# A shift for the softmax: from a row of bounds, made by matmuls of their own, to sixteen rows of the scores' contraction

## The chip, the core and the metric

The kernel runs on one core of one Trainium2 chip, with one launch. The metric is the device time of one execution in microseconds (us). The kernel before took 1345.86 us (median of 3 runs, 1345.21 to 1346.31).

## What is computed

One block mixes two branches over the same input x (2048 tokens, 512 channels) by a gate per token:

```python
x = A_x
g = sigmoid((x * gate_w).sum(-1, keepdims=True))
# branch A: attention, H = 32 heads of Dh = 16
q, k, v = split_heads(x @ wqkv)
p = softmax(einsum("bhqd,bhkd->bhqk", q, k) * Dh ** -0.5)
a = (p @ v, heads joined) @ wo
# branch B: an MLP over the token axis
h = layernorm(x)
b = (gelu(h^T @ w1 + b1) @ w2 + b2)^T        # hidden width F = 1792
out = g * a + (1 - g) * b
```

Everything is float32 with a float32 result. The kernel gets that precision from a faster float format by splitting each operand in a high and a low part and adding three products: high by high, high by low, low by high.

## The kernel before

**Stages.** The program runs five stages after each other, each of them a stretch of the profile.

1. *v and the gate* (0 to 65 us). Tiles of x are loaded, transposed on TensorE, split (`turn`) and multiplied with the v columns of `wqkv`. The gate comes from a row sum on VectorE.
2. *Projection* (65 to 153 us). For each of four blocks b of 128 channels (8 heads), `project` makes k and then q, transposed: 128 channels by 512 tokens in one PSUM bank, 12 matmuls each (L72), for n = 0 to 3. So there are 32 units: 16 of k and 16 of q. `parts` splits each unit in `pc` (ScalarE copies the high part, VectorE subtracts for the low part) and stores both planes to DRAM (`kp`, `qp`; `pc` has three buffers). In between, VectorE makes the layer norm of eight tiles of x for branch B (`ln_load`, `ln_scale`, `ln_rows`).
3. *First layer of the MLP* (153 to 314 us): `layer` (L360), with weights split just ahead of their use on ScalarE and GpSimd, and `gelu` on VectorE and ScalarE.
4. *Attention* (319 to 1290 us), with the second MLP layer and the output projection woven in. The order of all engines is written out by hand here. A group is a pair of heads by half of the queries: 32 groups, some 30 us each. A group has 11 phases (`ph`). In one phase TensorE makes six scores (`score`, L706: 128 keys by 512 queries), beside them up to six matmuls of the dense work (`dn`, L744), and then 24 products with v of the phase before (`apply_v`, L673). ScalarE turns two scores at a time into exponentials (L715). VectorE takes finished `dn` banks out (L442, L551), takes the finished sum of a group out (`evacuate`), and divides attention outputs (`divide` in `fetch_o`: it waits for the loads `o_lo` and `o_sum`, L527 and L528). There is a single bank for `dn` and a single one for `av`.
5. *The end* (1290 to 1345 us): the last output rows.

**Scores.** A score contracts the stacked planes of one head in one half of the 128 rows (`HALF` = 64): 16 rows each of high k by high q, high k by low q and low k by high q (`PAIRS`). One row more (`C_ROW`) takes a shift off, so that no exponential overflows without a look at the scores themselves: on the side of k this row holds ones, on the side of q the shift of each query, 49 rows in all.

**The shift.** It is a bound of what a query can reach with any key: minus 1.01 times the sum over the head's 16 channels of |q| times the greatest |k| of the channel. `kmax` (L312) holds the greatest |k| for each channel of a block, `km` (L315) places it in one column per head, `qa` (L322) is |q| in bf16, and `bound` (L294 to L301) multiplies the two on TensorE: 128 rows, 8 heads, 512 queries, one matmul for each q unit (L296). VectorE copies the 8 by 512 result to `cb` (L297) and reduces its least value into `far` (L299); `cb` goes to DRAM as `cd`. Bounds run late: a list `late` keeps them back until three are waiting, and `last_bounds` does the rest after the first block of the MLP's first layer. `far` then gives a flag (L343 to L348) that decides at the very end (L816) whether a slow general softmax has to run instead; it doesn't on these inputs.

**Loads in attention.** `load_q` (at phase 0) and `load_k` (at phase 1) fetch the next group's operands into two buffers each: six DMAs of 128 KB for k (`ks<-kp`, L422), six of 64 KB for q (`qs<-qp`, L422) and two of 4 KB for the shift (`qs<-cd`, L437). All are issued by SyncE (SP) in program order, with every other load and store of the kernel in the same queue: the weights (`w_raw`, L133), outputs of a group (`o`, L647, and `r`, L657), `o_lo` and `o_sum`, and rows of branch B (`row`, L547). The rows of ones in the two k buffers are set once by four memsets on VectorE (L413), just ahead of the first attention loads.

The order in stages 1 to 3 is made by a scheduler from program order and data dependences; an instruction's place on its engine can thus move when others go.

Of the kernel before, what the change touches and what calls it, by code (L numbers as in the profile page):

```python
# [21 lines left out]
P = 128  # L22
# [19 lines left out]
PAIRS = [(0, 0, 0), (DH, 0, 1), (2 * DH + 1, 1, 0)]  # L42
C_ROW = 2 * DH
ROWS = DH * len(PAIRS) + 1
# [13 lines left out]
def gated_mix(ctx: ExitStack, tc: tile.TileContext, a_x, a_wqkv, a_wo, b_w1, b_b1, b_w2, b_b2, gate_w, out):  # L58
# [18 lines left out]
    qp_d = [dram.tile([2, P, S], F32, name=f"qp{b}") for b in range(ND)]  # L77
    kp_d = [dram.tile([2, P, S], F32, name=f"kp{b}") for b in range(ND)]
    c_d = [dram.tile([P // DH, S], F32, name=f"cd{b}") for b in range(ND)]
# [12 lines left out]
    far = const.tile([P // DH, ND * NQ], F32, name="far")  # L92
# [187 lines left out]
    with tc.tile_pool(name="ln0", bufs=3, side="right") as ln:  # L280
# [8 lines left out]
        def parts(ps, dst, n):  # L289
            pc = qk.tile([P, 2, NB], F32R, name="pc", bufs=3)  # L290
            split(pc[:, 0, :], pc[:, 1, :], ps, nc.scalar.copy, nc.vector.tensor_tensor)
            nc.sync.dma_start(dst[:, :, n * NB : (n + 1) * NB].rearrange("c p t -> p c t"), pc.bitcast(F32))

        def bound(b, n, km, qa, cb):  # L294
            pc = bank()[: P // DH]
            nc.tensor.matmul(pc, km, qa, start=True, stop=True)  # L296
            nc.vector.tensor_copy(cb[:, n * NB : (n + 1) * NB], pc)  # L297
# [5 lines left out]
        late = []  # L303
        for b in range(ND):
            wk_b, wq_b = qk_w.pop(0), qk_w.pop(0)
            kmax = bd.tile([P, NQ], F32, name="kmax")
            for n in range(NQ):
# [3 lines left out]
                parts(ps, kp_d[b], n)  # L311
                nc.vector.tensor_reduce(kmax[:, n : n + 1], ps, axis=AX.X, op=ALU.max, apply_absolute_value=True)  # L312
            nc.vector.tensor_reduce(kmax[:, 0:1], kmax, axis=AX.X, op=ALU.max)
            km = bd.tile([P, P // DH], BF16, name="km")
            nc.vector.tensor_scalar(km, head_of, kmax[:, 0:1], BOUND_SLACK, ALU.mult, ALU.mult)  # L315
            cb = bd.tile([P // DH, S], F32R, name="cb", bufs=1)
            for n in range(NQ):
                ps = project(wq_b, n)
                while len(late) > 2:
                    bound(*late.pop(0))  # L320
# [573 lines left out]
```

## Time and profile before

| | us |
|---|---|
| median of 3 runs | 1345.86 |
| the profiled execution | 1346.53 |
| its span, first to last instruction | 1344.7 |
| busy ScalarE (ACT) | 1093.5 |
| busy VectorE (DVE) | 421.2 |
| busy GpSimd (POOL) | 202.2 |
| TensorE weight loads (PEld, beside matmuls) | 773.1 |
| TensorE clock granted, mean | 0.997 of full speed |
| DMA moved | 133.16 MB, 99 GB/s over the span |

All terms of the prediction are taken from the profiled execution, which is 0.67 us above the median of the runs.

How to read the rows: in a view of *groups*, a row is a line of the code, an engine, an operation, its output and inputs by name, shapes and a count, then the busy time in us with the mean of one in ns, then the engine's idle time ahead of it and what ended that. In a *timeline* a row starts with the start and the duration in us; an idle time and its releaser stand in brackets at the end. SPq rows are DMA issues, not transfers. Matmuls overlap: one of 512 columns is shown with 0.39 us, and the next starts 0.23 us after it. A row of *windows* gives for a stretch the busy time of PE, PEld, DVE, ACT and POOL with instruction counts, then the granted clock, the share of the 16 DMA engines that was busy, and GB/s.

### The profile page before, as it was taken

The numbers are of one execution on the slowest core, as the hardware profiler recorded it, in microseconds if no ns is written. First come the engines' busy times: TensorE is split into PE (matmuls) and PEld (weight loads), VectorE is DVE, ScalarE is ACT, GpSimd is POOL, SyncE is SP. The second block draws the span as 40 slices with busy tenths as digits, with TensorE's granted clock in tenths as the row PEclk, the third lists the DMA queues.
The fourth block names the chain that finished last, engine by engine and source line by source line (L and its number), as shares of the span: only waits on it lengthen the run. The fifth ranks groups of instructions, "written<-read, shape, count | busy, mean of one in ns | idle before, by whom it ended". The sixth has DMA issues, their size and how long they took to land.

```text
span 1344.7 us, 32450 instructions
## 1 busy us (share of the span) xinstructions
PE 1321.9 (98%) x13302; PEld 773.1 (57%) x13302; DVE 421.2 (31%) x637; ACT 1093.5 (81%) x1264; POOL 202.2 (15%) x458
## 2 busy tenths in 40 slices
PE   8999999999999999999999999999999999999996
PEld 6877788876555555555555555555555555554543
DVE  3596663444321111112322111232111122333223
ACT  3353244446999999999999999999999999999994
POOL 0210144443110111111100111100111111100001
PEclk9999999999999999999999999999999999999998
DMA  3565443326432333333555332454333333456411
GB/s 117 164 235 207 169 142 94 94 63 150 88 76 53 73 69 60 71 67 64 115 120 125 80 78 46 102 131 116 69 69 62 73 69 64 90 127 177 93 29 66
DMA packets 90776, 133.16 MB, mean 99 GB/s; under 512 B 13381, under 2 KB 52443, under 8 KB 87515
## 3 DMA queue, kind: packets, MB, share of 16 engines
q1 hardware_dynamic: 90186, 130.21, 39.7%
q8 instruction: 107, 1.75, 0.6%
q10 hardware_dynamic: 432, 0.79, 0.2%
q14 instruction: 51, 0.41, 0.1%
HBM read 97.01 MB, written 33.94 MB: 97 GB/s over the span
## 4 chain that ended last, share of the span: by engine, by line
PE 91%; issue 4%; ACT 1%; DVE 1%; DMA 1%; POOL 0%; SPq 0%; POOLq 0%; DVEq 0%; ACTq 0%
PE av L673 33%; PE s L706 26%; PE acc L360 11%; PE acc L72 10%; PE dn L744 10%; ACT pt L715 1%; DMA o_sum<-r 1%; PE acc L184 1%; PE acc L296 0%; DVE ks L413 0%; DMA wv_raw<-in_A_wqkv_dram 0%; POOL base L805 0%; SPq L422 0%; DVE o_sum L531 0%; POOL w_lo L65 0%
## 5 line engine op out<-in xcount | busy, mean ns | idle before, releaser
L715 ACT ACTIVATE pt<-s 128x1024 f32<-128x1024 f32 x1024 | 965.0, 1031 | 38.8 <-PE s L706 33.1
L706 PE MATMUL s<-qs,ks 49*128 49x512 f32 x2048 | 530.9, 421 | 4.0 <-ACT pt L715 4.0
L673 PE MATMUL av<-pt,v 128*17 128x256 f32 x8192 | 510.6, 381 | 0.1
L706 PEld LDWEIGHTS s<-qs,ks 49*128 49x128 f32 x2048 | 303.8, 184 | 208.5 <-ACT pt L715 157.2
L673 PEld LDWEIGHTS av<-pt,v 128*17 128x17 f32 x8192 | 205.2, 97 | 258.5 <-issue 124.4
L744 PE MATMUL dn<-u_hi,w_hi 64*128 64x512 f32 x432 | 186.1, 431 | 0.6 <-POOL token L748 0.6
L65 POOL TENSOR_TENSOR w_lo<-w_raw,w_hi 128x512 fp32r<-128x512 f32 (+1 forms) x128 | 155.1, 1215 | 143.4 <-ACT w_hi L64 113.3
L744 PE MATMUL dn<-u_lo,w_hi 64*128 64x512 f32 x432 | 171.2, 396 | 0.0
L744 PE MATMUL dn<-u_hi,w_lo 64*128 64x512 f32 x432 | 169.7, 393 | 0.0
L748 POOL MEMSET token<- 1x1 f32 x310 | 28.3, 91 | 848.6 <-PE dn L744 584.7
L639 DVE COPY ot<-av 128x512 f32<-128x512 f32 x32 | 22.1, 691 | 354.8 <-PE av L673 354.8
L652 DVE RECIPROCAL rt<-rt 128x512 f32<-128x512 f32 x31 | 103.9, 3353 | 1.1
L64 ACT CAST w_hi<-w_raw 128x512 fp32r<-128x512 f32 (+1 forms) x67 | 37.9, 567 | 69.7 <-PE acc L360 63.7
L360 PE MATMUL acc<-h_hi,w_lo 128*128 128x512 f32 x224 | 88.7, 396 | 0.3 <-POOL w_lo L65 0.3
L360 PE MATMUL acc<-h_hi,w_hi 128*128 128x512 f32 x224 | 88.9, 397 | 0.0
L360 PE MATMUL acc<-h_lo,w_hi 128*128 128x512 f32 x224 | 88.6, 395 | 0.0
L744 PEld LDWEIGHTS dn<-u_hi,w_lo 64*128 64x128 f32 x432 | 79.8, 185 | 5.2
L744 PEld LDWEIGHTS dn<-u_hi,w_hi 64*128 64x128 f32 x432 | 79.5, 184 | 4.8 <-POOL token L748 1.0
L744 PEld LDWEIGHTS dn<-u_lo,w_hi 64*128 64x128 f32 x432 | 80.0, 185 | 2.5
L64 DVE CAST w_hi<-w_raw 128x512 fp32r<-128x512 f32 (+1 forms) x61 | 22.5, 378 | 116.0 <-PE dn L744 79.6
L442 DVE TENSOR_SCALAR row<-dn,b2x,omg 128x512 f32<-128x512 f32 x16 | 12.9, 809 | 126.9 <-PE dn L744 105.9
L72 PE MATMUL acc<-xt_hi,wc_hi 128*128 128x512 f32 x128 | 51.2, 400 | 0.0
(133 smaller groups left out, 1076.7 us busy)
## 6 DMA issues: line engine op xcount, KB each, us to landing
w_raw<-in_B_w_dram SPq DMA_DIRECT2D x96, 256.0 KB
ks<-kp SPq DMA_DIRECT2D x192, 128.0 KB
qs<-qp SPq DMA_DIRECT2D x192, 64.0 KB
x<-in_A_x_dram SPq DMA_DIRECT2D x32, 256.0 KB
kp<-pc SPq DMA_DIRECT2D x16, 512.0 KB
qp<-pc SPq DMA_DIRECT2D x16, 512.0 KB
w_raw<-in_B_w_dram SPq DMA_DIRECT2D x32, 128.0 KB
bp<-row SPq DMA_DIRECT2D x16, 256.0 KB
```

What stands on the lines that cost most here:

```text
L64: copy(hi, src)
L65: sub(lo, src, hi.bitcast(F32), ALU.subtract)
L72: nc.tensor.matmul(ps, a, b, start=start and n == 0, stop=stop and n == last)
L184: nc.tensor.transpose(pt[:, k, :], xs[t][:, k * P : (k + 1) * P], ident)
L360: nc.tensor.matmul(p, a, b, start=first and k == 0, stop=last and k == 2)
L639: nc.vector.tensor_copy(ot, av)
L652: nc.vector.reciprocal(rt, rt)
L673: nc.tensor.matmul(av[32 * j : 32 * j + VC, i * QC : (i + 1) * QC], v[:, c, g % NP * 2 + i, :], pt[:, h * QC : (h + 1) * QC], start=added[ ...
L706: nc.tensor.matmul(s[:, m, :], kt[grp][rows, c * P : (c + 1) * P], qt[grp][rows, qb * NB : (qb + 1) * NB], start=True, stop=True,)
L715: nc.scalar.activation(pt, s, AF.Exp, scale=SCALE)
L744: mm = nc.tensor.matmul(ps, a[half], b[half], start=first and not second, stop=last and bool(second))
L748: fence = nc.gpsimd.memset(token, 0.0)
```

## The change

The row of ones and the row of shifts go. The three pairs of planes take 48 rows, and 16 rows more (`SHIFT`) hold |q| on the side of q and the greatest |k| of the channel, times -1.01, on the side of k, the same value for all keys. So the score's own contraction takes the shift off: 64 rows in place of 49, a full half.

- In the projection, `bound` and its 16 matmuls go, with `qa`, `cb`, `cd` and the list `late`. |q| becomes a third plane of `pc` and `qp`: ScalarE writes it there in the same activation (Abs), after VectorE's low part, and the store of a q unit grows from 512 KB to 768 KB. VectorE reduces the greatest |q| of each channel (`qmax`), 128 by 512 from PSUM, once for each q unit.
- For each block, VectorE scales `kmax` and spreads it to 128 by 512 (`km`), which is stored to DRAM (256 KB).
- The flag is made from `most` (greatest |q| times greatest |k| for each channel and block) by two small matmuls in `least_shifts`, in the place of `last_bounds`: 8 by 4 and 1 by 4. TensorE gets to the first of them 14 matmuls into the MLP's first layer, and to the second 2 full matmuls later.
- In attention, `load_k` issues two DMAs more, 128 KB each, which repeat 2 KB of `km` four times in each of 16 rows; `load_q` fetches the third plane by two DMAs of 64 KB in the place of the two of 4 KB. The k buffers come from the pool like the q buffers; the four memsets go.
- The general softmax reads the same planes as before.

```diff
-PAIRS = [(0, 0, 0), (DH, 0, 1), (2 * DH + 1, 1, 0)]
-C_ROW = 2 * DH
-ROWS = DH * len(PAIRS) + 1
+PAIRS = [(0, 0, 0), (DH, 0, 1), (2 * DH, 1, 0)]
+SHIFT = (3 * DH, 2, 2)
+ROWS = 4 * DH
...
-        def parts(ps, dst, n):
-            pc = qk.tile([P, 2, NB], F32R, name="pc", bufs=3)
+        def parts(ps, dst, n, m):
+            pc = qk.tile([P, 3, NB], F32R, name="pc", bufs=3)[:, :m, :]
             split(pc[:, 0, :], pc[:, 1, :], ps, nc.scalar.copy, nc.vector.tensor_tensor)
+            if m == 3:
+                nc.scalar.activation(pc[:, 2, :], ps, AF.Abs)
             nc.sync.dma_start(dst[:, :, n * NB : (n + 1) * NB].rearrange("c p t -> p c t"), pc.bitcast(F32))
 
-        def bound(b, n, km, qa, cb):
-            pc = bank()[: P // DH]
-            nc.tensor.matmul(pc, km, qa, start=True, stop=True)
-            nc.vector.tensor_copy(cb[:, n * NB : (n + 1) * NB], pc)
-            i = b * NQ + n
-            nc.vector.tensor_reduce(far[:, i : i + 1], pc, axis=AX.X, op=ALU.min)
-            if n == NQ - 1:
-                nc.sync.dma_start(c_d[b], cb.bitcast(F32))
+        def greatest(dst, ps):
+            nc.vector.tensor_reduce(dst, ps, axis=AX.X, op=ALU.max, apply_absolute_value=True)
...
             nc.vector.tensor_reduce(kmax[:, 0:1], kmax, axis=AX.X, op=ALU.max)
-            km = bd.tile([P, P // DH], BF16, name="km")
-            nc.vector.tensor_scalar(km, head_of, kmax[:, 0:1], BOUND_SLACK, ALU.mult, ALU.mult)
-            cb = bd.tile([P // DH, S], F32R, name="cb", bufs=1)
+            nc.vector.tensor_scalar_mul(kmax[:, 0:1], kmax[:, 0:1], BOUND_SLACK)
+            km = bd.tile([P, NB], F32R, name="km")
+            nc.vector.tensor_copy(km, kmax[:, 0:1].broadcast_to([P, NB]))
+            nc.sync.dma_start(km_d[b], km.bitcast(F32))
             for n in range(NQ):
                 ps = project(wq_b, n)
-                while len(late) > 2:
-                    bound(*late.pop(0))
-                qa = bd.tile([P, NB], BF16, name="qa", bufs=4)
-                nc.scalar.activation(qa, ps, AF.Abs)
-                parts(ps, qp_d[b], n)
-                late.append((b, n, km, qa, cb))
+                parts(ps, qp_d[b], n, 3)
+                greatest(qmax[:, n : n + 1], ps)
...
+            nc.vector.tensor_reduce(qmax[:, 0:1], qmax, axis=AX.X, op=ALU.max)
+            nc.vector.tensor_mul(most[:, b : b + 1], qmax[:, 0:1], kmax[:, 0:1])
...
-    def last_bounds():
-        while late:
-            bound(*late.pop(0))
-
-        nc.vector.tensor_scalar(far, far, -BOUND_LIMIT, None, ALU.is_lt)
-        pf = bank()[:1, : ND * NQ]
+    def least_shifts():
+
+        ps = bank()
+        nc.tensor.matmul(ps[: P // DH, :ND], head_of, most, start=True, stop=True)
+        far = bd.tile([P // DH, ND], F32, name="far")
+        nc.vector.tensor_scalar(far, ps[: P // DH, :ND], -BOUND_LIMIT, None, ALU.is_lt)
+        pf = bank()[:1, :ND]
         nc.tensor.matmul(pf, ones[: P // DH, :], far, start=True, stop=True)
...
-    k_bufs = [stk.tile([P, S], F32R, name=f"ks{i}", bufs=1) for i in range(2)]
-    for t in k_bufs:
-        for i in range(2):
-            nc.vector.memset(t[i * HALF + C_ROW : i * HALF + C_ROW + 1].bitcast(F32), 1.0)
-
-    def stack(dst, src, which, pair, cols):
+    def stack(dst, src, which, pair, cols, planes):
         b, r0 = divmod(pair * 2 * DH, P)
         for i in range(2):
-            for row, *part in PAIRS:
+            rows = slice(r0 + i * DH, r0 + (i + 1) * DH)
+            for row, *part in planes:
                 at = slice(i * HALF + row, i * HALF + row + DH)
-                rows = slice(r0 + i * DH, r0 + (i + 1) * DH)
                 nc.sync.dma_start(dst[at].bitcast(F32), src[b][part[which], rows, cols])
+            if which:
+                at = slice(i * HALF + SHIFT[0], i * HALF + SHIFT[0] + DH)
+                shift = km_d[b][rows][:, None, :].broadcast_to([DH, NQ, NB])
+                nc.sync.dma_start(dst[at].bitcast(F32).rearrange("r (n c) -> r n c", c=NB), shift)
 
     def load_k(g):
-        t = k_bufs[g % 2]
-        stack(t, kp_d, 1, g % NP, slice(0, S))
+        t = stk.tile([P, S], F32R, name="ks")
+        stack(t, kp_d, 1, g % NP, slice(0, S), PAIRS)
         return t
 
     def load_q(g):
...
-        stack(t, qp_d, 0, pair, cols)
-        b, h0 = divmod(pair * 2, P // DH)
-        for i in range(2):
-            at = i * HALF + C_ROW
-            nc.sync.dma_start(t[at : at + 1].bitcast(F32), c_d[b][h0 + i : h0 + i + 1, cols])
+        stack(t, qp_d, 0, pair, slice(half * QW, (half + 1) * QW), [*PAIRS, SHIFT])
         return t
```

More of the change, by code (lines that the diff above doesn't have):

```diff
@@ L91, in gated_mix @@
     omg = const.tile([P, NS], F32, name="omg")
-    far = const.tile([P // DH, ND * NQ], F32, name="far")
+    most = const.tile([P, ND], F32, name="most")
     flag = const.tile([1, 1], I32, name="flag")
@@ L394, in gated_mix @@
                 if f0 == 0 and c == 0:
[L395 removed]
+                    least_shifts()
                 if f0 == 0 and c == 1:
@@ L813, in gated_mix @@
     att_ctx.close()
-    far_off = nc.values_load(flag, min_val=0, max_val=(P // DH) * ND * NQ, skip_runtime_bounds_check_because="a count")
+    far_off = nc.values_load(flag, min_val=0, max_val=H, skip_runtime_bounds_check_because="a count")
     with tc.If(far_off != 0):
```

22 lines of the change are left out of this document (9 added, 13 removed).

## The prediction

> **What bounds the kernel now.** I read the page's busy times first, then the chain of work that ended last, then the groups, and last the timeline at the places where the change acts.
>
> ```profile
> span 1344.7 us, 32450 instructions
> PE 1321.9 (98%) x13302; PEld 773.1 (57%) x13302; DVE 421.2 (31%) x637; ACT 1093.5 (81%) x1264; POOL 202.2 (15%) x458
> PE av L673 33%; PE s L706 26%; PE acc L360 11%; PE acc L72 10%; PE dn L744 10%; ACT pt L715 1%; DMA o_sum<-r 1%; PE acc L184 1%; PE acc L296 0%; DVE ks L413 0%; DMA wv_raw<-in_A_wqkv_dram 0%; POOL base L805 0%; SPq L422 0%; DVE o_sum L531 0%; POOL w_lo L65 0%
> ```
>
> TensorE is busy for 98% of the span, and the chain runs nearly always through it. So a matmul that goes is worth its slot, and work on another engine is free unless TensorE comes to wait for it. The chain has small links that the change touches: the bounds (L296), the memsets (L413), and a load (`o_sum`).
>
> **The bounds go.** First what one costs, from the timeline of TensorE in the projection:
>
> ```profile
> 80.83 0.39 PE L72 MATMUL acc<-xt_hi,wc_lo 128*128 128x512 f32 x1
> ...
> 81.15 0.38 PE L296 MATMUL acc<-qa,km 128*8 128x512 bf16 x1
> ...
> 81.46 0.50 PE L72 MATMUL acc<-xt_hi,wc_hi 128*128 128x512 f32 x1
> ...
> 81.80 0.40 PE L72 MATMUL acc<-xt_lo,wc_hi 128*128 128x512 f32 x1
> ...
> 82.03 0.39 PE L72 MATMUL acc<-xt_hi,wc_lo 128*128 128x512 f32 x1
> ```
>
> The undisturbed pitch is 0.23 us (81.80 to 82.03). From 80.83 to 82.03 lie 1.20 us with three full matmuls, 0.69 us, so one bound takes 0.51 us, twice its place, because the matmuls on both sides of it start late as well. Thirteen of the sixteen stand alone like this: 13 x 0.51 = 6.6 us. Three stand together after the first block of the MLP's first layer:
>
> ```profile
> 155.83 0.40 PE L360 MATMUL acc<-h_hi,w_lo 128*128 128x512 f32 x1
> 156.16 0.81 PE L296 MATMUL acc<-qa,km 128*8 128x512 bf16 x3
> 156.90 0.50 PE L360 MATMUL acc<-h_hi,w_hi 128*128 128x512 f32 x1
> 157.24 0.40 PE L360 MATMUL acc<-h_lo,w_hi 128*128 128x512 f32 x1
> ```
>
> From 155.83 to 157.24 lie 1.41 us with two full matmuls, 0.46 us: the three cost 0.95 us. **Term 1: -7.6 us**, on the path, as TensorE has no idle time in this stage (44.00 busy of 44.00 in the row of windows further down).
>
> **VectorE and ScalarE.** These are not on the path here.
>
> ```profile
> L297 DVE CAST cb<-acc 8x512 fp32r<-8x512 f32 x16 | 10.8, 673 | 7.8 <-PE acc L296 6.4 <-DMA cd<-cb 1.4
> ...
> L312 DVE TENSOR_REDUCE kmax<-acc 128x1 f32<-128x512 f32 x16 | 10.8, 677 | 0.0
> ...
> L322 ACT ACTIVATE qa<-acc 128x512 bf16<-128x512 f32 x16 | 9.5, 595 | 15.9 <-PE acc L72 15.9
> ```
>
> `qmax` has the shape of `kmax`, 677 ns x 16, and replaces the copy alone (673 ns x 16); the reduction to `far` goes on top, and four copies to `km` come. ScalarE's Abs stays and only writes another tile. What hides all this are eight PSUM banks ahead of TensorE; without them VectorE's order would cost time. The memsets stand in the chain too:
>
> ```profile
> 310.42 1.76 DVE L413 MEMSET ks<- 1x2048 f32 x1 [0.47 <-issue]
> ...
> 311.48 0.39 PE L360 MATMUL acc<-h_hi,w_lo 128*128 128x512 f32 x1
> ...
> 312.21 1.41 DVE L368 TENSOR_SCALAR gu<-acc,b 128x512 f32<-128x512 f32 x2
> ```
>
> The first `gu` needs the bank that was finished at 311.48 + 0.39 and so could start 0.3 us earlier. I take 0, as the start of attention is set by loads (below), and -0.3 as the bound.
>
> **The flag's matmuls.** One small matmul becomes two.
>
> ```profile
> 162.14 0.39 PE L360 MATMUL acc<-h_lo,w_hi 128*128 128x512 f32 x1
> ...
> 162.59 0.50 PE L360 MATMUL acc<-h_hi,w_lo 128*128 128x512 f32 x1
> 162.93 0.39 PE L360 MATMUL acc<-h_hi,w_hi 128*128 128x512 f32 x1
> ```
>
> The present one costs 0.79 - 0.46 = 0.33 us; one more costs the same. The first now waits for `most`, behind which all of TensorE's queue stands. Its chain from the last projection's end: ScalarE's high part, VectorE's low part, ScalarE's Abs, VectorE's `qmax` and two tiny operations. At 0.60 us an operation for ScalarE (L322) and 0.68 for VectorE (L312) these are 2.6 us; with some 0.3 us for the tiny ones and 0.39 us until the last matmul is through, that is 3.3 us and some handovers; TensorE gets there after 14 matmuls x 0.23 = 3.2 us. I take 0.2 us, with bounds of 0 and 1. The second small matmul has two full matmuls and its neighbour's delay to cover one tiny VectorE operation: nothing. **Term 2: +0.5 us.**
>
> **The scores.** A score gets 64 rows in place of 49.
>
> ```profile
> L706 PE MATMUL s<-qs,ks 49*128 49x512 f32 x2048 | 530.9, 421 | 4.0 <-ACT pt L715 4.0
> L706 PEld LDWEIGHTS s<-qs,ks 49*128 49x128 f32 x2048 | 303.8, 184 | 208.5 <-ACT pt L715 157.2
> ...
> L744 PEld LDWEIGHTS dn<-u_hi,w_lo 64*128 64x128 f32 x432 | 79.8, 185 | 5.2
> ```
>
> The dense work beside the scores has 64 rows already: its weights load in 185 ns against 184, and on the timeline the two kinds of matmul start together, 0.23 us apart. So nothing, from 0 to 1 ns x 2048 = 2 us if the load were exposed, which it isn't.
>
> **The loads.** Here the change pays. Each group loads 2 x 131 kB more for k and 2 x 62 kB more for q, 12 MB over the 32 groups. Most of it is far from any wait, since operands are asked for a whole group, some 30 us, ahead. The places that matter are those where TensorE stands behind a transfer that now queues behind the new ones.
>
> ```profile
> 65.00:109.00 44.00, 44.00 (x188) 33.84 (x187) 40.38 (x117) 20.91 (x44) 5.92 (x4) 1.00 0.71 247
> ...
> 308.00:318.00 10.00, 8.80 (x39) 6.89 (x38) 9.14 (x11) 4.51 (x8) 5.55 (x5) 1.00 0.87 171
> 668.00:685.00 17.00, 16.91 (x206) 8.66 (x208) 4.38 (x4) 16.81 (x19) 1.82 (x7) 1.00 0.78 154
> ```
>
> From 668 to 685 the engines moved 154 GB/s at a share of 0.78: 197 GB/s at full share. The two new k loads, 262 kB, then take 1.3 us of a queue that is full. That is my price per place, between 0 (other transfers leave room) and 2.2 us (0.9 us of SP's time for two issues, as six take 2.73 us below, comes on top).
>
> First place, the second fetch of attention outputs:
>
> ```profile
> 669.52 2.73 SPq L422 DMA_DIRECT2D ks<-kp  x6
> ...
> 684.37 1.22 DVE L531 TENSOR_TENSOR o_sum<-o_lo,o_sum 128x1024 f32<-128x1024 f32 x1 [12.59 <-DMA o_sum<-r]
> ...
> 688.46 0.47 PE L744 MATMUL dn<-wo_hi,o_hi 64*128 64x512 f32 x1 [0.58 <-DVE row L442]
> ```
>
> VectorE waits 12.59 us for `o_sum`, issued right behind the k loads. Behind it in VectorE's queue stands L442, which empties the one `dn` bank, and TensorE waits for that already. So a later landing goes straight to the end: +1.3 us. Second place, the same for the other half of the queries:
>
> ```profile
> 1186.87 1.23 DVE L531 TENSOR_TENSOR o_sum<-o_lo,o_sum 128x1024 f32<-128x1024 f32 x1 [11.83 <-DMA o_sum<-r]
> ...
> 1190.00 0.80 DVE L442 TENSOR_SCALAR row<-dn,b2x,omg 128x512 f32<-128x512 f32 x1
> ...
> 1191.18 0.39 PE L744 MATMUL dn<-wo_hi,o_hi 64*128 64x512 f32 x1
> ```
>
> L442 ends at 1190.80 and TensorE needs it at 1191.18, so 0.4 us are free: +0.9 us. Third place, an output row loaded behind the k loads:
>
> ```profile
> 895.33 0.75 DVE L551 SCALAR_TENSOR_TENSOR row<-dn,g,row 128x512 f32<-128x512 f32 x1 [1.15 <-DMA ks<-kp]
> ...
> 896.62 0.50 PE L744 MATMUL dn<-wo_hi,o_hi 64*128 64x512 f32 x1
> ```
>
> L551 is released by a DMA and ends 0.5 us before TensorE needs the bank: +0.8 us. I found no other place where a load is the last thing that TensorE waits for, and count nothing more. Fourth place, the start of attention:
>
> ```profile
> 316.28 0.69 SPq L437 DMA_DIRECT2D qs<-cd  x2
> ...
> 319.41 0.49 PE L706 MATMUL s<-qs,ks 49*128 49x512 f32 x1
> ...
> 322.39 0.49 PE L744 MATMUL dn<-u_hi,w_hi 64*128 64x512 f32 x1 [0.64 <-POOL token L748]
> ```
>
> The first score starts 2.4 us after the last q load's issue, and now 262 + 123 kB more come ahead of it, 2.0 us at 171/0.87 = 197 GB/s. About half a microsecond of that had been free, and TensorE then waits for a GpSimd token at 322.39 anyway, which takes some 0.8 us more: +0.5 us, from 0 to 1.4. **Term 3: 1.3 + 0.9 + 0.8 + 0.5 = +3.5 us.**
>
> The Trainium skill speaks for a smaller price here: "DMA: Bandwidth & Descriptors", Specifications, gives about 358 GB/s per core from HBM, by which the same 262 kB take 0.7 us and term 3 would be some 1.5 us, with a time of 1340.2 us. The trace's own 197 GB/s, with rows of 16 partitions in flight, is the lower rate, and I keep to it.
>
> **The sum.** -7.6 + 0.5 + 3.5 = -3.6 us on the profiled execution (span 1344.7 us; 1346.53 us with what lies around it): 1342.9 us. The median of the runs is 0.67 us lower, so the forecast is **1342.2 us**.
>
> **Rivals.**
>
> *The new loads are hidden.* For it: a share of 0.78 leaves room. Against: at 688.46 TensorE already waits behind such a load. Then only terms 1 and 2 count, -7.1 us: 1338.8 us.
>
> *They cost the full price.* SP's issue time adds to the transfer: 2.2 + 1.8 + 1.7 + 1.4 = 7.1 us in the four places, which eats the gain: 1345.9 us, no change.
>
> *The projection comes to wait for its stores (slower).* A q unit's store is half as large again, and `pc` has three buffers, so a unit may hold one for 3 x 12 x 0.23 = 8.3 us.
>
> ```profile
> 102.56 2.16 SPq L292 DMA_DIRECT2D qp<-pc  x2
> ...
> 109.28 0.59 ACT L64 CAST pc<-acc 128x512 fp32r<-128x512 f32 x1 [2.72 <-DMA qp<-pc]
> ```
>
> The store that released this buffer was the second of the two, issued by 104.7, so it took at least 4.6 us to land; 1.5 times that is 6.9 us, and with three operations of 0.6 to 0.7 us ahead of the issue a unit holds its buffer for 8.8 us: 0.2 us per unit too long, which the k units (5 + 1.3 us) and the banks make up. Bytes fit as well: 247 GB/s at a share of 0.71 is 348 GB/s at most, and this stretch would ask for 10.9 + 2.5 MB in 41 us, 327 GB/s. It decides from a hold of about 11 us: then q units come every 3.7 us, 16 us late in sum, of which the k units make up 10; with 1 us more at `most`, 7 us: 1349 us.
>
> *The change doesn't do what it says.* If the flag rose, the general softmax would run and the time would be a multiple. The flag needs a sum over 16 channels of |q||k| above 156; the inputs' spreads give q and k a deviation of 0.05 x 0.05 x sqrt(512) = 0.06, so the sum stays near 1.
>
> **How the numbers follow.** The forecast with terms 2 and 3 within about 1.5 us: 0.50, of which two thirds lie beyond 0.2% (below 1343.2 us; 0.2%, 2.7 us, is about what a measurement of this kernel can tell from no change). Loads hidden: 0.21, all faster. Full price: 0.16, mostly no change. Projection: 0.12, slower; the flag 0.01. So faster 0.55, same 0.29, slower 0.16. The likeliest case alone spans 1340.5 to 1344; the range reaches from the hidden loads less 1 us (the memsets, and no wait for `most`), 1337.8, to just beyond the full price, 1346.8.
>
> **What would show it.** Right: no L296; the 12 matmuls of every projection unit 2.7 us apart; the first layer starting 6 to 7 us earlier; scores unchanged near 421 ns; waits before L744 at the two fetches longer by about 1 us each. Wrong: idle time of TensorE ahead of L72, or ScalarE waiting often for `qp<-pc` (projection rival); the fetches unchanged (hidden loads); waits for the k or q loads at the start of groups, or a clock below 1.00 in attention, neither of which I count at all.

## The result: slower by 0.67%, and the profile after

| | before | changed | |
|---|---|---|---|
| median, 6 runs each (us) | 1346.03 | 1354.28 | forecast 1342.2, range 1337.8 to 1346.8 |
| all runs (us) | 1345.21 to 1346.94 | 1353.31 to 1358.0 | |
| ratio, 95% interval | | 1.0067 [1.0053, 1.0081] | slower |
| profiled execution, span (us) | 1344.7 | 1352.0 | +7.3 |
| mean granted clock | 0.997 | 0.992 | |

The forecast had the sign wrong. First the page of the changed kernel: its span, the busy times, and the chain of work that ended last, by engine.

```profile
span 1352.0 us, 32495 instructions
PE 1321.1 (98%) x13288; PEld 775.5 (57%) x13288; DVE 406.7 (30%) x629; ACT 1095.4 (81%) x1264; POOL 201.6 (15%) x458
...
PE 86%; DMA 4%; issue 4%; SPq 3%; ACT 1%; DVE 1%; POOL 0%; POOLq 0%; DVEq 0%; ACTq 0%
```

TensorE is as busy as before (1321.1 us against 1321.9) in a span 7.3 us longer. In the chain of work, TensorE's share falls from 91% to 86%; the DMA links grow from 1% to 4% and the DMA issues (SPq) from 0% to 3%. The view of TensorE's waits says where they come in. The columns are the total in us, the number of waits, and the longest.

```profile
PE dn L733 <- DVE row L431: 5.3, 2, 3.2
...
PE dn L733 <- DVE row L540: 2.1, 2, 1.2
PE dn L733 <- POOL token L737: 1.6, 1, 1.6
PE s L695 <- DMA qs<-qp: 1.1, 1, 1.1
```

These six waits come to 10.1 us; in the kernel before, the waits of the same kinds were 0.6 us for the second-layer row and 0.6 for the token. (The token is a 1 by 1 write by GpSimd, behind which the next phase's first dense matmul may start; in GpSimd's order it stands behind the split of weights. L431, L520, L540, L695, L733, L737 of the changed kernel are L442, L531, L551, L706, L744, L748 of the kernel before.)

**Where the time went.** Both kernels put the same 1632 dense matmuls (`dn`, with 64 rows) beside the scores, in the same order. So I set the start of the n-th of them in the one timeline against the n-th in the other. The difference only moves where something happened, which splits the loss better than any view of sums.

| the same matmul, start in the kernel before (us) | 319 | 343 | 685 | 708 | 723 | 904 | 1186 | 1208 | 1222 | 1289 |
|---|---|---|---|---|---|---|---|---|---|---|
| changed minus before (us) | -6.97 | -4.42 | -4.64 | +0.91 | +2.24 | +2.52 | +2.39 | +4.91 | +6.54 | +6.88 |

The changed kernel comes into attention 7 us early and leaves it 7 us late. In the long stretches (343 to 685, 723 to just ahead of 904, 904 to 1186) the difference stays within 0.3 us: 64 rows in a score and 12 MB more traffic cost nothing there. The 13.9 us are lost at six places, a few us long each: 2.6 at the start, 5.5 at the first fetch, 1.35 at a row soon after it, 0.3 at a row at 903, 2.5 at the second fetch, 1.6 at a row after that.

The gain in the projection is as forecast. These are the rows of TensorE's first layer in the changed kernel and then before, with first and last start:

```profile
L355 PE MATMUL acc<-h_hi,w_hi x224: 388/397/400, 146.3 to 305.0; 128*128 128x512 f32 x112
```

```profile
L360 PE MATMUL acc<-h_hi,w_hi x224: 388/393/502, 153.2 to 311.7; 128*128 128x512 f32 x112
```

It starts 6.9 us earlier. The projection has no stall in this stretch, at 280 GB/s in place of 247 (windows of the changed kernel):

```profile
65.00:109.00 44.00, 44.00 (x196) 36.44 (x195) 39.26 (x118) 20.62 (x43) 4.38 (x3) 1.00 0.80 280
```

What comes between there and the first score nearly cancels. The same matmul of the first layer is 7.55 us early behind the three late bounds and 6.66 us early at the end of the layer. Then TensorE is early by 8.1 us, because a wait of the kernel before is gone. First that wait, from the view of waits of the kernel before:

```profile
PE dn L691 <- ACT gs L369: 1.2, 1, 1.2
```

Then the last matmul ahead of the first score, in the kernel before and in the changed one:

```profile
319.09 0.39 PE L691 MATMUL dn<-u_hi,w_lo 128*128 128x512 f32 x1
```

```profile
310.97 0.39 PE L680 MATMUL dn<-u_hi,w_lo 128*128 128x512 f32 x1
...
312.44 0.47 PE L695 MATMUL s<-qs,ks 64*128 64x512 f32 x1 [1.08 <-DMA qs<-qp]
```

The first score then waits 1.08 us for its q loads, and 7.0 are left. No run tells why the layer gives 0.9 us back, or why the wait for `gs` is gone (it is gone in e7 too, which keeps the four memsets).

**The first fetch, in the timeline.** SyncE issues the k loads, now eight (the last four are shown), and the fetch behind them:

```profile
667.66 1.35 SPq L412 DMA_DIRECT2D ks<-kp  x3
...
669.05 0.42 SPq L416 DMA_DIRECT2D ks<-km  x1
...
669.52 0.42 SPq L516 DMA_DIRECT2D o_lo<-o  x1
...
669.99 0.61 SPq L517 DMA_DIRECT2D o_sum<-r  x1
...
682.36 1.23 DVE L520 TENSOR_TENSOR o_sum<-o_lo,o_sum 128x1024 f32<-128x1024 f32 x1 [15.20 <-DMA o_sum<-r]
...
685.49 0.81 DVE L431 TENSOR_SCALAR row<-dn,b2x,omg 128x512 f32<-128x512 f32 x1
...
686.44 0.76 PE L733 MATMUL dn<-wo_hi,o_hi 64*128 64x512 f32 x1 [3.19 <-DVE row L431]
...
687.00 0.62 PE L733 MATMUL dn<-wo_lo,o_hi 64*128 64x512 f32 x1
```

TensorE waits 3.19 us in place of 0.58. That is 2.6 of the 5.5 us lost here. The rest is in the durations: this matmul takes 0.76 us and the next 0.62 us, where 0.47 and 0.39 are usual. The windows of the changed kernel, one behind the other, tell why. The third figure from the end is the granted clock.

```profile
682.61:686.02 3.41, 0.64 (x5) 0.18 (x1) 3.34 (x4) 0.81 (x1) 0.00 (x0) 1.00 0.00 0
686.02:689.43 3.41, 2.99 (x15) 2.10 (x19) 0.61 (x2) 2.10 (x3) 1.27 (x1) 0.50 0.49 154
689.43:692.85 3.42, 3.42 (x28) 1.48 (x22) 0.00 (x0) 0.76 (x1) 0.09 (x1) 0.50 0.00 0
692.85:696.26 3.41, 3.41 (x46) 1.65 (x48) 0.75 (x1) 3.09 (x4) 0.09 (x1) 1.00 0.18 67
```

After a window with 0.64 us of work the clock is at 0.50 for 6.8 us, and 2.9 us are lost while TensorE is "busy". At the start of attention it happens again: the clock is at 0.50 from 317.4 to 320.8, and of the 2.6 us lost there about 1.6 are the clock's.

**A row behind the k loads.** Here TensorE waits for an output row whose load stands behind the eight k loads:

```profile
707.66 0.38 SPq L536 DMA_DIRECT2D row<-bp  x1
...
715.73 0.75 DVE L540 SCALAR_TENSOR_TENSOR row<-dn,g,row 128x512 f32<-128x512 f32 x1 [7.00 <-DMA row<-bp]
...
716.62 0.46 PE L733 MATMUL dn<-wo_hi,o_hi 64*128 64x512 f32 x1 [0.86 <-DVE row L540]
```

The load is issued at 707.66 and VectorE gets on at 715.73. In the kernel before, the same row found its data there: VectorE's idle time ahead of that operation was ended by TensorE.

```profile
704.96 0.43 SPq L547 DMA_DIRECT2D row<-bp  x1
...
713.07 0.75 DVE L551 SCALAR_TENSOR_TENSOR row<-dn,g,row 128x512 f32<-128x512 f32 x1 [5.26 <-PE dn L744]
```

### The profile page after: what moved, and what is told of

Read it like the earlier page. It is cut to its first block, busy times and chain, and to the rows that moved or that the text cites. A ratio compares the mean times of both kernels' runs of the same rounds, so it can differ in the third digit from the quotient of the medians.

```text
span 1352.0 us, 32495 instructions
## 1 busy us (share of the span) xinstructions
PE 1321.1 (98%) x13288; PEld 775.5 (57%) x13288; DVE 406.7 (30%) x629; ACT 1095.4 (81%) x1264; POOL 201.6 (15%) x458
## 4 chain that ended last, share of the span: by engine, by line
PE 86%; DMA 4%; issue 4%; SPq 3%; ACT 1%; DVE 1%; POOL 0%; POOLq 0%; DVEq 0%; ACTq 0%
PE av L662 31%; PE s L695 24%; PE acc L355 11%; PE acc L73 10%; PE dn L733 9%; DMA o_sum<-r 2%; SPq L412 2%; DMA row<-bp 1%; ACT pt L704 1%; PE acc L185 1%; SPq L636 0%; DMA ks<-km 0%; DMA ks<-kp 0%; DVE o_sum L520 0%; DMA wv_raw<-in_A_wqkv_dram 0%
## 5 line engine op out<-in xcount | busy, mean ns | idle before, releaser
L695 PE MATMUL s<-qs,ks 64*128 64x512 f32 x2048 | 533.8, 422 | 5.1 <-ACT pt L704 4.0
L695 PEld LDWEIGHTS s<-qs,ks 64*128 64x128 f32 x2048 | 305.0, 185 | 212.0 <-ACT pt L704 154.0
L733 PE MATMUL dn<-u_hi,w_hi 64*128 64x512 f32 x432 | 186.2, 431 | 1.6 <-POOL token L737 1.6
L733 PE MATMUL dn<-u_lo,w_hi 64*128 64x512 f32 x432 | 171.2, 396 | 0.0
L733 PE MATMUL dn<-u_hi,w_lo 64*128 64x512 f32 x432 | 169.8, 393 | 0.0
L737 POOL MEMSET token<- 1x1 f32 x310 | 28.4, 92 | 860.2 <-PE dn L733 520.0
L733 PEld LDWEIGHTS dn<-u_hi,w_hi 64*128 64x128 f32 x432 | 79.4, 184 | 4.2 <-POOL token L737 1.9
L733 PEld LDWEIGHTS dn<-u_lo,w_hi 64*128 64x128 f32 x432 | 79.9, 185 | 3.2
L733 PEld LDWEIGHTS dn<-u_hi,w_lo 64*128 64x128 f32 x432 | 79.8, 185 | 3.0
L733 PE MATMUL dn<-wo_hi,o_hi 64*128 64x512 f32 x112 | 48.2, 430 | 7.8 <-DVE row L431 5.3
L431 DVE TENSOR_SCALAR row<-dn,b2x,omg 128x512 f32<-128x512 f32 x16 | 13.0, 810 | 128.5 <-PE s L695 64.5
```

The lines of the kernel that those rows point to most:

```text
L695: nc.tensor.matmul(s[:, m, :], kt[grp][rows, c * P : (c + 1) * P], qt[grp][rows, qb * NB : (qb + 1) * NB], start=True, stop=True,)
L733: mm = nc.tensor.matmul(ps, a[half], b[half], start=first and not second, stop=last and bool(second))
L737: fence = nc.gpsimd.memset(token, 0.0)
```

## The experiments

The theory, "queue": the new loads stand ahead of urgent ones in SyncE's one queue, at the fetches and at rows loaded soon after the k loads; VectorE's order hands the delay to TensorE; and a stall halves the clock on top. Rivals: "everywhere" (64 rows, or traffic in sum), SyncE's issue time in place of bytes, and loads that only hurt because TensorE came earlier. The table gives the timed runs, with the difference of the same matmul to the kernel before at places of the table above; e8 and e10 are one execution each and follow further down. In the kernels of the runs the line numbers are shifted by a few, so the rows are to be read by their names.

| run | median (us) | ratio, 95% interval | at 319 | 343 | 685 | 708 | 1186 | 1208 | 1289 |
|---|---|---|---|---|---|---|---|---|---|
| changed | 1354.28 | 1.0067 [1.0053, 1.0081] | -6.97 | -4.42 | -4.64 | +0.91 | +2.39 | +4.91 | +6.88 |
| e1: no km loads | 1343.80 | 0.9983 [0.9973, 0.9993] | -5.93 | -3.07 | -3.24 | -2.87 | -3.03 | -3.05 | -3.03 |
| e2: nor those of \|q\| | 1342.88 | 0.9974 [0.9963, 0.9986] | -5.47 | -2.94 | -3.03 | -2.57 | -2.57 | -2.52 | -2.53 |
| e3: km loads tiny | 1344.12 | 0.9982 [0.9972, 0.9992] | -6.96 | -6.02 | -6.14 | -3.51 | -3.59 | -3.62 | -3.63 |
| e4: fetches first | 1344.82 | 0.9994 [0.9984, 1.0003] | -6.27 | -3.57 | -3.76 | -4.80 | -3.73 | -3.76 | -0.73 |
| e5: no shift rows | 1341.93 | 0.9969 [0.9956, 0.9982] | -8.04 | -5.34 | -5.56 | -5.32 | -5.47 | -5.49 | -5.45 |
| e6: loads spread | 1342.00 | 0.9964 [0.9950, 0.9977] | -5.52 | -3.01 | -3.24 | -4.27 | -4.42 | -4.45 | -4.41 |
| e7: before, no bounds | 1345.13 | 0.9989 [0.9979, 0.9999] | -4.13 | +0.15 | +0.15 | +0.14 | +0.15 | +0.14 | +0.14 |
| e9: before, two loads more | 1357.29 | 1.0071 [1.0055, 1.0087] | +0.64 | +3.13 | +3.10 | +6.05 | +6.18 | +9.86 | +12.79 |
| e11: e6, weights first | 1344.67 | 0.9981 [0.9971, 0.9991] | -4.07 | -3.11 | -2.54 | -3.50 | -2.71 | -2.67 | -2.66 |

**e1: the km loads away.**

```diff
-            if which:
+            if which and shifts:
...
-        t = stk.tile([P, S], F32R, name="ks")
-        stack(t, kp_d, 1, g % NP, slice(0, S), PAIRS)
+        t = k_bufs[g % 2]
+        stack(t, kp_d, 1, g % NP, slice(0, S), PAIRS, g < 2)
```

> The changed kernel with the shift rows of k loaded for the first two groups only, into two fixed buffers; all later groups use those rows, so their shifts are not their own heads'. 60 of the 64 loads of km are gone, all else stays. Theory 'queue' (the new loads stand ahead of urgent loads in SP's queue at five places, and a long stall halves TensorE's clock for some us on top): the two fetches lose nearly all of their 5.5 and 2.5 us, the row loads after them most of 1.35 and 1.6 us, the start keeps its 2.6 us: 1354.3 - 9.5 = 1345 us (1343 to 1347). Rival 'everywhere' (64 rows a score, or the traffic as such, slow the whole of attention): 1352 to 1354 us, as scores and most of the traffic stay.

Measured: 1343.80 us. Between 343 and the end the difference moves by 0.04 us, where the changed kernel lost 11.3. All that was lost behind the start comes from these 60 loads, and none of it from the 64 rows, which this run has. Its stall at the first fetch (timeline of e1):

```profile
685.60 0.47 PE L735 MATMUL dn<-wo_hi,o_hi 64*128 64x512 f32 x1 [0.95 <-DVE row L433]
```

0.95 us, and no half clock behind it.

**e2: the loads of |q| away too.** This comes on top of the edit of e1.

```diff
-        t = stk.tile([P, QW], F32R, name="qs")
-        stack(t, qp_d, 0, pair, slice(half * QW, (half + 1) * QW), [*PAIRS, SHIFT])
+        t = q_bufs[g % 2]
+        stack(t, qp_d, 0, pair, slice(half * QW, (half + 1) * QW), [*PAIRS, SHIFT] if g < 2 else PAIRS)
```

> As the run before, and |q| too is loaded for the first two groups only (two fixed buffers for q), so later groups use the first ones' |q|. Theory 'queue': only the start's 2.6 us stay of the 13.9: 1354.3 - 11.3 = 1343 us (1341.5 to 1344.5); what this run gains over the one before is the share of |q|, 1 to 3 us. Rival 'everywhere': 1350 to 1353 us.

Measured: 1342.88 us. The intervals of e1 and e2 overlap, and at the first fetch the difference moves by 0.46 us, no less than in e1 (0.37). The larger loads of |q| cost nothing that can be seen there; I had expected 1 to 3 us.

**e3: issue or bytes.**

```diff
+                else:
+                    nc.sync.dma_start(dst[at, :4].bitcast(F32), km_d[b][rows, :4])
```

> As the first run, but the two loads of km of every later group are still issued, at their place, with 16 x 4 elements (256 bytes) in place of 16 x 2048. It tells the issue from the bytes. If SP's time for two more issues is what counts (0.84 us a group): the first fetch is still late enough to stall TensorE for some 1.5 to 2.5 us, 1348 to 1352 us. If the 262 kB count: within 1 us of the first run, 1345 us.

Measured: 1344.12 us, the time of e1. But the timeline shows that the issue alone is not free at the first fetch:

```profile
683.38 0.47 PE L738 MATMUL dn<-wo_hi,o_hi 64*128 64x512 f32 x1 [1.63 <-DVE row L436]
```

The wait moves the matmuls by 1.06 us, against 0.37 in e1 and 2.62 in the changed kernel. So the price of the two loads at this place, 2.25 us, is some 0.7 us of issue and 1.55 us of bytes. (These are differences of single executions; e5, which has none of the new loads, moves by 0.24 us here, so they are good to a quarter of a us.) (The other 1.6 us that e3 loses here are the clock, which fell at 684.7; at its start it stayed at 1.00, so it ends near e1.) At the second fetch and the rows e3 loses nothing: there it is bytes.

**e4: the second fetch of each half one step earlier.**

```diff
-            call(at - 3, fetch_o, 0, 1)
+            call(at - 4, fetch_o, 0, 1)
...
-    call(at - 3, fetch_o, 1, 1)
+    call(at - 4, fetch_o, 1, 1)
```

> The changed kernel, complete, with the second fetch of each half called one step earlier, so that its two loads are issued ahead of that group's k loads and not behind them. Theory 'queue': the waits of TensorE for the second-layer row at the two fetches vanish, and with the first of them the halved clock: -5.5 - 0.6 (the stall that was there before the change) and -2.5 us; the start and the two row loads stay: 1354.3 - 8.6 = 1345.7 us (1344 to 1348). Rival 'bytes' (the fetch is late because the engines are full, wherever it is issued): 1350 to 1353 us. Rival 'everywhere': as the changed kernel less 1 us at most.

Measured: 1344.82 us. Both fetches lose nothing any more (the first gains 1.0, since the stall of the kernel before goes as well). The rows behind the k loads still lose, 0.9 us at the first (708 to 723), 1.9 at the second (by 1222) and 1.1 at two more after it. At the fetches the order in the queue decides, not the sum of the bytes.

**e5: no shift rows at all.** Neither km nor |q| is loaded, and a score has 48 rows; the projection still makes and stores both.

```diff
-            if which:
+            if which and False:
...
-        stack(t, qp_d, 0, pair, slice(half * QW, (half + 1) * QW), [*PAIRS, SHIFT])
+        stack(t, qp_d, 0, pair, slice(half * QW, (half + 1) * QW), PAIRS)
...
-            rows = slice(i * HALF, i * HALF + ROWS)
+            rows = slice(i * HALF, i * HALF + 3 * DH)
```

> The changed kernel with the shift left out of the scores: neither the km loads nor the loads of |q| in any group, the first one included, and scores of 48 rows in place of 64. The projection still computes and stores |q| and km. Theory 'queue': the gain of the first part stays whole and nothing is lost in attention: first score about 7 to 8 us earlier than in the kernel before, and the same at the end, 1346.0 - 7.5 = 1338.5 us (1337 to 1340.5). Rival 'the gain is not there' (the projection or the first layer gives part of it back later): 1341 us or more.

Measured: 1341.93 us, 3.4 us above what I expected and in the range of the rival, though nothing is lost from 343 on. Part of the gain is given back, partly as the rival had it: 1.5 us in the first layer (from -8.12 to -6.58), which the missing wait for `gs` makes good again, and 2.7 us at the start of attention, where -8.04 becomes -5.34 without any of the new loads. VectorE's operation behind the last `gelu` there (`u_lo`), first in the kernel before and then, with what follows it, in e5:

```profile
318.74 1.83 DVE L65 TENSOR_TENSOR u_lo<-gu,u_hi 128x512 fp32r<-128x512 f32 x2
```

```profile
311.86 1.83 DVE L66 TENSOR_TENSOR u_lo<-gu,u_hi 128x512 fp32r<-128x512 f32 x2
...
313.62 0.41 DVE L65 CAST w_hi<-w_raw 128x512 fp32r<-128x512 f32 x1
...
314.16 1.26 POOL L66 TENSOR_TENSOR w_lo<-w_raw,w_hi 128x512 fp32r<-128x512 f32 x1 [1.62 <-DVE w_hi L65]
...
315.51 0.49 PE L733 MATMUL dn<-u_hi,w_hi 64*128 64x512 f32 x1 [1.45 <-POOL token L737]
```

TensorE had come 8 us earlier, but the last `gelu` and the weights' split behind it on VectorE only 6.9. So 1.2 us are given back to VectorE's queue, and 1.5 to the clock (0.50 from 316.1 to 319.5). Of the changed kernel's loss at the start only about 1 us is the loads' (-4.4 against -5.3).

**e6: the loads spread.** All 16 loads of a group stay, two at a time over eight phases.

```diff
-                nc.sync.dma_start(dst[at].bitcast(F32), src[b][part[which], rows, cols])
+                todo.append((dst[at].bitcast(F32), src[b][part[which], rows, cols]))
...
+    def load_some(n):
+        for dst, src in todo[:n]:
+            nc.sync.dma_start(dst, src)
+        del todo[:n]
...
                 if ph == 0 and grp + 1 < NG:
                     qt[grp + 1] = load_q(grp + 1)
-                if ph == 1 and grp + 1 < NG:
                     kt[grp + 1] = load_k(grp + 1)
+                load_some(2)
```

> The changed kernel, complete, with the 16 loads of a group (8 of k, 8 of q) issued two at a time in the group's first eight phases, in place of 8 in each of the first two. Same bytes, same count. Theory 'queue': no urgent load has more than two of them ahead of it, so the losses at the fetches and the row loads go (11.3 us) and the start's 2.6 us stay, more or less by the clock: 1342 us (1340 to 1344), which is below the kernel before. Rival 'bytes in sum': nothing gained, 1352 to 1354 us.

Measured: 1342.00 us, 0.9964 [0.9950, 0.9977] of the kernel before, with the computation complete: the fastest complete version of these runs, and as fast as e5, which has no such loads. Some 1.0 us of the 4.4 is not the shift rows' gain: at the first fetch the difference falls from -3.24 to -4.27, as the stall of the kernel before goes too. The kernel before with its own loads spread was not run. The rows of its waits that are left at the start of attention are these; the view has no row any more for the second-layer row or for an output row.

```profile
PE dn L741 <- POOL token L745: 1.6, 1, 1.6
PE s L703 <- DMA qs<-qp: 1.3, 1, 1.3
```

**e7: the gain by itself.** In the kernel before, the bounds' matmuls are left out (shift and count are constants).

```diff
-            nc.tensor.matmul(pc, km, qa, start=True, stop=True)
-            nc.vector.tensor_copy(cb[:, n * NB : (n + 1) * NB], pc)
+            nc.vector.memset(cb[:, n * NB : (n + 1) * NB].bitcast(F32), -1.0)
```

> The kernel before with the 16 matmuls for the bounds left out (a constant shift of -1 and a count of zero are written in their place), so all loads and 49 rows stay as they were. It measures term 1 of the prediction alone: -7.6 us, 1338.4 us (1337.5 to 1339.5). If matmuls of 8 columns cost their plain slot only (0.23 us each), -3.7 us, 1342.3 us.

Measured: 1345.13 us, far less gain than either figure. The first layer does start 6.1 us earlier, at 147.1 in place of 153.2. That is 0.47 us for each of the thirteen bounds ahead of it, near the 0.51 of term 1 and not the 0.23 of a plain slot. Then it waits for weights, and the clock falls (timeline and windows of e7):

```profile
183.61 0.50 PE L358 MATMUL acc<-h_hi,w_hi 128*128 128x512 f32 x1 [1.20 <-ACT w_hi L64]
...
184.97 0.51 PE L358 MATMUL acc<-h_hi,w_lo 128*128 128x512 f32 x1 [0.62 <-POOL w_lo L65]
```

```profile
182.63:186.04 3.41, 1.80 (x7) 1.19 (x8) 0.69 (x1) 1.97 (x4) 2.40 (x2) 1.00 0.04 7
186.04:189.45 3.41, 3.41 (x10) 2.63 (x9) 0.00 (x0) 0.62 (x1) 1.73 (x3) 0.50 0.66 188
```

What was left went at the start of attention, with the token and 6.8 us of half clock. So this run does not measure term 1 at the end; it shows that 6 us won at 150 us need not arrive there.

**e8 and e10: the clock without the loads.** In the kernel before, VectorE does the last step of one `divide` three times (e8) or four times (e10), which delays the row and moves no load.

```diff
             split(hi, lo, rb, nc.vector.tensor_copy, nc.vector.tensor_tensor)
+            for _ in range(2 if (half, k) == (0, 1) else 0):
+                nc.vector.tensor_tensor(lo, rb, hi.bitcast(F32), ALU.subtract)
```

> The kernel before with the last operation of VectorE's divide at the second fetch of the first half (the low part of the attention output, 1.23 us) done three times in place of once: no load moves, but the second-layer row stands 2.46 us later, so TensorE's stall there becomes 0.58 + 2.46 = 3.04 us, near the 3.19 us of the changed kernel. It tells the clock from the loads. If a stall of this length itself halves TensorE's clock afterwards: the granted clock falls to 0.50 for some 4 to 7 us behind it and the shift of all later matmuls is 4.5 to 6 us. If the slow matmuls after the stall came from the loads: the clock stays at 1.00 and the shift is 2.5 us.

Measured (one execution, 1348.97 us): a stall of 2.77 us, and the clock stayed at 1.00. The matmuls behind are 2.2 us late, by which the stall is longer, and no more. By itself that spoke for the loads as the cause of the half clock, so I took all runs together. In each execution every change of the granted clock lies on one grid of 3.413 us: in the changed kernel 317.38, 320.78, 686.02, 692.84 and 1341.38, which are 0, 1, 108, 110 and 300 steps. In e8 a grid line (counted back from its drop at 1337.82, at the end) cuts the stall in halves, and both windows still have some 2 us of work:

```profile
685.88:689.29 3.41, 1.97 (x27) 0.79 (x25) 3.31 (x4) 2.15 (x3) 0.09 (x1) 1.00 0.00 0
689.29:692.70 3.41, 2.08 (x23) 1.53 (x27) 1.51 (x3) 1.49 (x2) 1.39 (x2) 1.00 0.40 103
692.70:696.11 3.41, 3.41 (x52) 1.86 (x46) 0.75 (x1) 3.09 (x4) 0.09 (x1) 1.00 0.13 51
```

> As the run with the longer wait (2.77 us of stall, and a clock that stayed at 1.00), with the low part done four times: the stall becomes 2.77 + 1.23 = 4.0 us. In the runs so far every change of the clock lies on one grid of 3.413 us per execution, and the clock fell where at least 1.63 us of one such window were idle and stayed where at most 1.49 us were. A stall of 4.0 us cannot be cut by such a grid into pieces below 2 us. If that is the rule: the clock falls to 0.50 for one or two windows (3.4 or 6.8 us), and the later matmuls are 3.4 + 1.7 to 3.4 = 5.1 to 6.8 us late. If the clock in the changed kernel fell for another reason (the loads): 3.4 us late and 1.00.

Measured (one execution, 1350.80 us): a stall of 3.69 us, a little less than the 4.0 expected, and this time the clock falls, as the rule had it. The windows of e10:

```profile
688.75:692.16 3.41, 1.07 (x10) 1.02 (x11) 2.50 (x4) 0.47 (x1) 0.80 (x1) 1.00 0.11 40
692.16:695.57 3.41, 3.41 (x29) 1.05 (x25) 0.00 (x0) 2.39 (x3) 0.58 (x2) 0.50 0.42 114
695.57:698.98 3.41, 3.41 (x42) 1.96 (x40) 0.75 (x1) 2.49 (x3) 0.09 (x1) 1.00 0.00 0
```

4.8 us are lost (5.1 to 6.8 were expected): 3.1 by the wait, the rest by the clock. No load was moved. So a stall by itself lowers the clock, and by these two executions its place on the grid decides whether it does.

**e9: the loads without the rest.** The kernel before gets two more loads of 123 kB behind each group's k loads, into rows that no score reads.

```diff
         stack(t, kp_d, 1, g % NP, slice(0, S))
+        b, r0 = divmod(g % NP * 2 * DH, P)
+        for i in range(2):
+            at = slice(i * HALF + ROWS, (i + 1) * HALF)
+            rows = slice(r0 + i * DH, r0 + i * DH + HALF - ROWS)
+            nc.sync.dma_start(t[at].bitcast(F32), kp_d[b][0, rows, :])
```

> The kernel before with two more loads of 15 rows x 8 kB (123 kB each) behind the six k loads of every group, into rows that no score reads; bounds, 49 rows and everything else stay. It adds the suspected cost without any other part of the change. Theory 'queue': the same places lose as in the changed kernel, 2.3 us at the first fetch (a stall of 2.9 us, with up to 2.9 us more if the clock halves), some 2 at the second, 1.3 and 1.5 at the row loads, 0.5 at the start: 1346.2 + 7.6 = 1353.8 us (1352 to 1357). Rival: the loads hurt only because TensorE came earlier in the changed kernel, so the same loads are hidden here: 1346 to 1348 us.

Measured: 1357.29 us, ratio 1.0071 [1.0055, 1.0087], just above the range that "queue" gave. The losses are at three of the expected places, 2.5 us at the start, 2.95 at the first fetch and 3.7 at the second; of these 1.6, 1.6 and 1.5 are the clock's. The first row load loses 0.14 us where 1.3 were expected, the second 1.2, and 1.6 more go to the clock behind 1236 us. In the rows of its waits are the same pairs:

```profile
PE dn L749 <- DVE row L447: 3.7, 2, 1.9
PE dn L749 <- POOL token L753: 1.6, 1, 1.6
...
PE dn L749 <- DVE row L556: 0.8, 1, 0.8
```

The clock fell four times from the start of attention on. The loads suffice to make the kernel slower; TensorE's earlier arrival isn't needed. But the price is not the same: at the first fetch the wait costs 1.35 us here and 2.6 in the changed kernel, for nearly the same bytes of k. These loads take rows of 8 kB, the loads of `km` pieces of 2 kB, and the q loads are smaller here; no run tells which of it makes the difference.

**e11: the start mended?** e6 with the first two weight loads between the k and the q loads of the first group, their high parts on ScalarE.

```diff
-        kt, qt = {0: load_k(0)}, {0: load_q(0)}
+        kt = {0: load_k(0)}
         load_some(len(todo))
...
-        for _ in range(2):
-            split_weight(nc.vector.tensor_copy)
+        qt = {0: load_q(0)}
+        load_some(len(todo))
+        for _ in range(2):
+            split_weight()
```

> The changed kernel with the spread loads, complete, and at the start of attention the two weight loads issued between the k and the q loads of the first group, their high parts copied by ScalarE in place of VectorE. Theory: TensorE's 1.6 us wait for the token there, which VectorE's queue and the late weights set, goes; the first score starts up to 1 us later, behind the weights in the queue. If the clock then stays at 1.00, the start's loss falls from 2.5 to about 1 us: 1340.3 us (1339 to 1342). If the longer single wait ahead of the first score halves the clock instead: 1342 us, the same as with the spread loads alone.

Measured: 1344.67 us, 2.7 us above e6 (the two intervals overlap) and above both figures expected. The token's wait is gone, but the q loads come later than I had thought:

```profile
315.34 0.76 PE L705 MATMUL s<-qs,ks 64*128 64x512 f32 x1 [3.82 <-DMA qs<-qp]
```

One wait of 3.82 us takes the place of two shorter ones, and the clock is at 0.50 for 6.8 us. The start's loss isn't mended by this order in the queue. What would mend it was not tried further.

## Why the prediction was wrong, point by point

- **Term 1 (bounds, -7.6): right as far as it goes.** The first layer was to start 6 to 7 us earlier and starts 6.9 earlier. That the first score comes 7.0 earlier, with 7.1 by terms 1 and 2, is luck: 0.9 us given back in the layer, a wait of 1.2 us gone and 1.1 us of waiting for q loads nearly cancel. What I didn't ask is whether the gain lasts: e5 gives back 2.7 us at the start of attention without any new load. Where TensorE comes earlier, the question is what is late next; there it was VectorE's last `gelu`.
- **Term 2 (flag, +0.5): +0.1.** The two small matmuls cost 0.21 and 0.20 us, and there is no wait for `most`.
- **Scores and VectorE: right.** The scores take 422 ns (421 before), and in the long stretches, some 800 us of attention, the difference moves by 0.3 us at most.
- **Term 3 (loads, +3.5) is the step that failed: +12.2.** That is 0.9 us at the start (-4.42 against -5.34 in e5) and the 11.3 lost behind it, which e1 doesn't lose. The other 1.7 of the 13.9 us are term 1's, which didn't last. The start's 0.9 is within the bounds that I gave it (0 to 1.4); the two fetches were the right places with sizes too small, the rows at 716 and 1222 us were missing, and so was the clock.
  - *The price.* I took 1.3 us, the bytes at 197 GB/s, and left SyncE's issue to the bound of 2.2. At the first fetch it is 2.25, both together (e1, e3): the bound, and the price of the full-price rival. (In e9 it is 1.35, so no one price holds for every load.) The waits at the two fetches moved TensorE by 2.6 and 2.5 us, forecast 1.3 and 0.9.
  - *The Trainium skill's rate.* "DMA: Bandwidth & Descriptors", Specifications, with a limit of about 358 GB/s per core, gave an estimate of 0.7 us for these bytes; the runs gave 1.55 us, 169 GB/s. The page was further off than the row.
  - *The places.* "I found no other place where a load is the last thing that TensorE waits for" was wrong for the rows at 716 and 1222 us, 1.35 and 1.6 us. The place of this kind that I did find (895) cost 0.3 in place of 0.8. I looked for rows that a DMA released already, and not for rows loaded behind the k loads with little time left.
  - *The clock.* "a clock below 1.00 in attention, neither of which I count at all": 2.9 us at the first fetch and 1.6 at the start, 4.5 us together: a third of the 13.9, and more than the forecast's whole gain. Without the new loads e1 and e5 keep the clock at 1.00 at the fetch, but e5 loses 1.5 us to it at the start all the same.
- **The rivals.** Hidden loads: refuted. Projection: refuted, with 44.00 us busy of 44.00. Full price: its 2.2 us was the better price, but without the rows and the clock it still came to "no change". Of the 0.16 for slower, 0.12 stood for the projection's stores; a fetch that stalls long enough to halve the clock was not among the rivals.

The sum by what was measured, by places: -7.0 at the first score; waits of 1.0 (start), 2.6 and 2.5 (fetches), 1.35, 0.3 and 1.6 (rows), which are 9.4 us; 4.5 us of half clock; +0.4 after attention. Together +7.3 us of span.

## What to carry to other kernels

A load that is early enough itself can still be late for the one behind it: where all DMAs share one queue, list for each added load what is issued within the next 10 us and which engine waits for that, whether or not it waits today. Spread such loads over the time that they have (e6: same bytes, 12 us less than the changed kernel), or put the urgent ones ahead. And a gain at one stage counts only when what meets it at the next stage came earlier too.

## What the runs showed of the hardware

The granted clock moved only between 1.00 and 0.50, on a grid of 3.413 us that runs through a whole execution (nine changes in e9, up to 300 steps apart, all within 0.01 of a step). In the thirteen profiled executions, up to the last output rows, 15 of 16 drops followed a window of the grid in which TensorE was busy for at most 1.84 of 3.41 us; of the windows with 1.88 us or more none was followed by a drop but one (2.48 us, in e9; I have no reason for it). The drops among the last output rows, one in each execution, are not in this count, and three of them fit less well: they followed windows with 2.07 us (e5), 2.19 us (e1) and 2.92 us (the changed kernel). A stall of 1.63 us inside one window halved the clock (e3), and one of 2.77 us cut by a grid line did not (e8). The Trainium skill, "TensorE: Matmul & The Clock Gate", Part 1, has the free-running window of 3413 ns, and the traces agree; it names an idle window as the condition for the lower clock, and here windows that were half idle were enough. That makes a stall's price depend on its phase: a wait of some 3 us cost nothing more in e8 (2.77 us) and 2.9 us more in the changed kernel (3.19 us). In the four runs of e9 the time follows the mean granted clock: 1354.03 us at 0.996, 1355.68 at 0.994, 1358.9 and 1359.38 at 0.992. So phase may be why these runs differ by 5.4 us (argued, not shown).
